# Another decoding of the float64 weights, and a new order of all steps, in a chunked-attention and gated-convolution kernel

## The chip, the cores and the metric

The kernel runs on one core of a Trainium2 chip. The core has five engines with a queue of instructions each: TensorE (PE, with its weight loads PEld), VectorE (DVE), ScalarE (ACT), GpSimd (POOL) and SyncE (SP, which only issues transfers). Each engine works through its queue in order and waits at an instruction until what it needs is there. Sixteen DMA engines move data between HBM and the core's memories. The metric is the device time of one execution in microseconds; lower is better.

## The reference

Two parts. The first is attention over q, k and v of shape (4 batches, 8 heads, 768 positions, 64). Each chunk of 32 queries sees 8 memory keys of its head, 16 keys to the left, its own 32 and 8 to the right, 64 in all. The second part takes the attention's output as x (4, 768, 512), makes a gate of a causal convolution with 5 taps and multiplies it with a matrix product:

```
scores = scale * q_c @ k_full.T;  a = exp(scores - max);  a = a / (sum(a) + 1e-9)
x[:, c] = a @ v_full                      # heads side by side: 512 columns
gate_pre = sum over k of conv_w[k] * x shifted by (4 - k) positions
out = (sigmoid(gate_pre) * (x @ w_val)) @ w_out
```

The inputs q, k, v, mem_k and mem_v are float32. The three weights w_val (512x512), conv_w (5x512) and w_out (512x512) are float64, so the kernel must make float32 values of them itself, from pairs of 32-bit words.

## The kernel before

**Units.** The attention is cut into 20 units: a unit is one pair of heads over one stretch of positions. Batch 0 has two stretches, of 256 and 512 positions (units 0 to 3 and 4 to 7); batches 1 to 3 have one of 768 each (units 8 to 11, 12 to 15, 16 to 19). For unit u the steps are: loads `lk`, `lq`, `lv`; transposes of k and q on PE (`tk`, `tq`) and their evictions (`ek`, `eq`); the scores (`sc`, PE, line 639); maximum, subtraction (`mx`, `ss`, DVE) and exponential (`ex`, ACT); transposes of the result (`tp`) and their evictions (`ep`); the product with v (`va`, PE, line 690); the division by the sum (`nd`, `ni`, `nx`, DVE, line 713 for `nx`); the transpose of the normalised x (`tx`); its split into a rounded part and the rest (`xh`, `xl`); five gate taps (`cv`, the first on ACT or DVE, lines 802 and 804, the others on DVE, line 798); and the tanh of the gate (`ga`, ACT). The tile of v is filled before its loads with the memory's rows (`mv`).

**Pieces.** The products with the weights go by 8 pieces of 256, 512 or 384 positions. `f1_n_co ci` is one block of x @ w_val of piece n, three matmuls (rounded x by rounded w, rounded x by the rest of w, the rest of x by rounded w; line 848). `h` (line 854) multiplies with the gate, `hh` and `hl` split the result, `f2_n_g ci` is one block of the product with w_out, again three matmuls (line 903), `oe` halves it and evicts it, and `st` stores it.

**Weights.** w_val and w_out come in four blocks of 128x512 float64 each, named wv0 to wv3 and wo0 to wo3, into two raw buffers (`lw`). Eight steps make a float32 block of a raw one: the exponent field (step 1, DVE, line 355), the mantissa field (2, DVE, 361), the low word added to it (3, DVE, 366), the exponent moved into place (4, ACT, 371), the mantissa as a number between 1 and 2 (5, ACT, 374), a clamp (6, DVE, 377), the sign (7, DVE, 382) and the product of both (8, POOL, 388). Then `h` makes the rounded part and the step without a suffix the rest. conv_w goes through the same eight steps once, as `cw1` to `cw8`.

**Order.** There is no scheduler at run time. A table, `ORDER`, lists every step with its engine (T is PE, V DVE, A ACT, G POOL, S SP), and the steps are emitted in this order; each engine's queue is what the table gives it. Buffers are counted, and a step that takes one waits for all users of the one that it replaces:

```
CAPS = dict(
    a=1, t=1, x=2, f=3, kn=2, qn=2, qT=2, ss=2, pT=2, xn=1, xh=4, xl=4, gate=5, h=2, hh=7, hl=7,
    o=3, ew=2, mw=2, wraw=2,
)
```

`wraw` is the raw weights, `ew` and `mw` the two work tiles of the decode, `kn` and `qn` the loaded k and q, `f` the PSUM banks of the products.

## Time and profile before

| | before |
|---|---|
| three timed runs, us | 267.76, 268.52 (median), 269.15 |
| span of the profiled execution, us | 269.1 |
| busy: PE, DVE, ACT, POOL, us | 238.3, 218.2, 127.9, 80.0 |
| instructions | 9694 |
| moved by DMA | 34.96 MB, mean 130 GB/s |

The span is the time from the first to the last instruction of one execution taken by the profiler; no other time of that execution is given, and the slowest of the timed runs is 0.05 us above it. The span is what a sum of durations is compared with, and it stands 0.6 us above the median of the timed runs.

Busy times are sums over the whole run, and this run has stages with different limits: DVE's share of the whole is 81%, and yet there are long stretches where it has no idle time, and others where it has much. So the windows are to be read, stage by stage. A group of instructions lists its count, its busy time and the mean of one. The chain follows the work that ended last back to what released it.

### The profile page before, as it was taken

Reading aid. Unit: us, or ns where it says so; the run is one execution under the profiler, and the core shown is the slowest. Engines: PE = TensorE matmul, PEld = TensorE weight load, DVE = VectorE, ACT = ScalarE, POOL = GpSimd, SP = SyncE. Lnnn points to the kernel's source line nnn. Section 1 sums busy time; section 2 is a strip of 40 time slices with the busy share of each in tenths; the row PEclk is TensorE's granted clock in tenths of the full one; section 3 lists DMA queues with packets and bytes.
Section 4 is the critical chain, followed back from the end, with each engine's and each line's share of the span. In section 5 each row is a group of like instructions: output and inputs, shape, how many; then the busy total and the mean of one; then the engine's idle time right before and its main releaser. Section 6 shows DMA issues by size and latency. Waiting matters only on the chain.

```text
span 269.1 us, 9694 instructions
## 1 busy us (share of the span) xinstructions
PE 238.3 (89%) x4158; PEld 200.2 (74%) x4158; DVE 218.2 (81%) x462; ACT 127.9 (48%) x259; POOL 80.0 (30%) x93
## 2 busy tenths in 40 slices
...
GB/s 151 177 198 207 211 178 183 117 210 180 177 137 147 144 186 178 44 132 137 165 164 132 160 149 55 106 163 187 101 143 2 4 168 44 80 0 39 78 48 111
DMA packets 99601, 34.96 MB, mean 130 GB/s; under 512 B 96082, under 2 KB 96358, under 8 KB 99558
## 3 DMA queue, kind: packets, MB, share of 16 engines
...
HBM read 28.03 MB, written 6.29 MB: 128 GB/s over the span
## 4 chain that ended last, share of the span: by engine, by line
PE 76%; DVE 12%; ACT 3%; issue 3%; DMA 3%; SPq 1%; POOL 1%; ACTq 0%; DVEq 0%
PE op L903 25%; PE vp L848 24%; PE sp L639 6%; PE xps L690 6%; PE tpx L750 4%; PE tq L569 4%; PE tk L569 4%; PE tp L569 4%; DVE gate L798 2%; DMA qn<-in_q_dram 2%; DVE e_wo L382 1%; DVE xn L713 1%; DVE e_wo L355 1%; SPq L493 1%; DMA craw<-in_moe_conv_w_dram 1%
## 5 line engine op out<-in xcount | busy, mean ns | idle before, releaser
L798 DVE SCALAR_TENSOR_TENSOR gate<-tpx,cw,gate 128x384 f32<-128x384 f32 (+9 forms) x144 | 79.3, 563 | 1.3 <-ACT gate L802 0.2
L264 POOL TENSOR_TENSOR hl<-h,hh 128x384 fp32r<-128x384 f32 (+2 forms) x25 | 26.0, 1044 | 107.6 <-DVE hh L249 55.2
L848 PE MATMUL vp<-xh,wv_hi 128*128 128x384 f32 (+2 forms) x128 | 49.1, 384 | 0.0
L848 PE MATMUL vp<-xl,wv_hi 128*128 128x384 f32 (+2 forms) x128 | 43.9, 343 | 0.0
L848 PE MATMUL vp<-xh,wv_lo 128*128 128x384 f32 (+2 forms) x128 | 43.9, 343 | 0.0
L903 PE MATMUL op<-wo_hi,hh 128*128 128x512 f32 (+1 forms) x100 | 41.9, 419 | 0.0
L903 PE MATMUL op<-wo_lo,hh 128*128 128x512 f32 (+1 forms) x100 | 38.6, 386 | 0.2 <-POOL wo_lo L264 0.2
L903 PE MATMUL op<-wo_hi,hl 128*128 128x512 f32 (+1 forms) x100 | 38.5, 385 | 0.0
L639 PE MATMUL sp<-kT,qT 64*32 64x64 f32 x1536 | 21.7, 239 | 8.7 <-DVE ss L664 3.9
L639 PEld LDWEIGHTS sp<-kT,qT 64*32 64x32 f32 x1536 | 17.6, 113 | 15.0 <-issue 8.4
L848 PEld LDWEIGHTS vp<-xh,wv_hi 128*128 128x128 f32 x128 | 25.0, 195 | 2.0
L854 DVE SCALAR_TENSOR_TENSOR h<-gate,vp 128x384 f32<-128x384 f32 (+2 forms) x32 | 17.2, 548 | 10.9 <-PE vp L848 9.4
L848 PEld LDWEIGHTS vp<-xh,wv_lo 128*128 128x128 f32 x128 | 25.1, 196 | 0.9
L848 PEld LDWEIGHTS vp<-xl,wv_hi 128*128 128x128 f32 x128 | 24.8, 194 | 0.9 <-DVE xl L264 0.2
L690 PE MATMUL xps<-v,pT 64*32 64x65 f32 x1536 | 21.1, 233 | 4.3 <-ACT pT L246 2.5
L690 PEld LDWEIGHTS xps<-v,pT 64*32 64x32 f32 x1536 | 17.3, 109 | 9.8 <-issue 6.1
L246 ACT COPY pT<-tp 128x384 f32<-128x384 f32 (+2 forms) x27 | 12.9, 479 | 23.5 <-PE tp L569 23.3
L569 PE MATMUL tk<-ident,kn 128*128 128x128 f32 x96 | 18.2, 304 | 6.2 <-ACT memT L246 2.6
L802 ACT ACTIVATE gate<-tpx,cw 128x384 f32<-128x384 f32 (+1 forms) x27 | 14.6, 549 | 15.1 <-PE tpx L750 10.0
L903 PEld LDWEIGHTS op<-wo_hi,hl 128*128 128x128 f32 x100 | 18.8, 188 | 4.0
L252 POOL COPY v<-mv 104x1536 f32<-104x1536 f32 (+2 forms) x12 | 17.4, 1458 | 11.5 <-issue 9.9
L569 PE MATMUL tq<-ident,qn 128*128 128x128 f32 x96 | 18.8, 311 | 2.1 <-DMA qn<-in_q_dram 0.9
...
## 6 DMA issues: line engine op xcount, KB each, us to landing
...
```

The lines of the kernel that those rows point to most:

```text
L246: return lambda: nc.scalar.copy(out(), in_())
L252: return lambda: nc.gpsimd.tensor_copy(out(), in_())
L264: return lambda: eng.tensor_tensor(out=out(), in0=a(), in1=b(), op=ALU.subtract)
L569: nc.tensor.transpose(U[name, i][:, (g - g0) * P : (g - g0 + 1) * P], src(g), ident)
L639: nc.tensor.matmul(U["sp"][CH * jc : CH * (jc + 1), j, g * WIN : (g + 1) * WIN], U["qT"][j * D : (j + 1) * D, g * P + CH * jc : g * P + CH ...
L690: nc.tensor.matmul(U["xps"][CH * jc : CH * (jc + 1), j, g * VW : (g + 1) * VW], U["pT"][j * D : (j + 1) * D, g * P + CH * jc : g * P + CH ...
L750: nc.tensor.transpose(U["x", i][:, o : o + P], U["xn"][:, g].rearrange("p j d -> p (j d)"), ident,)
L798: nc.vector.scalar_tensor_tensor(out=o, in0=i_, scalar=w, in1=o, op0=ALU.mult, op1=ALU.add)
L802: nc.scalar.activation(o, i_, AF.Copy, scale=w)
L848: nc.tensor.matmul(vp, w, x, start=ci == 0 and m == 0, stop=ci == NCT - 1 and m == 2)
L854: nc.vector.scalar_tensor_tensor(out=T["h", n, co][:, 0:nt], in0=bt[b, co]["gate"][:, t0 : t0 + nt], scalar=1.0, in1=T["vp", n, co][:, 0:n ...
L903: nc.tensor.matmul(op, x, w[:, ci, c0:c1], start=ci == 0 and m == 0, stop=ci == NCT - 1 and m == 2)
```

## The change

The decode has six steps in place of eight. The upper word of the float64, read as a float32, is scaled by a power of two and its absolute value is taken on ACT (`head`); two bounds are applied on DVE in one instruction; the bits are shifted left by 3 on DVE, which puts the exponent and the upper 20 bits of the mantissa in place; the sign is put in on DVE as before. The low word, scaled so that it fills the last three bits, is turned into an integer on ACT (`tail`) and added as an int32 on POOL. The two constant tiles and the steps `bias0` and `bias` are gone. What comes after the decode (`h`, the rest) is as it was.

```diff
+FLOOR = 2.0**-63
+CEIL = (1.875 - 2.0**-23) * 2.0**-32
...
-            nc.vector.tensor_scalar(
-                out=R["e"], in0=raw()[:, :, 1], scalar1=20, scalar2=0x7FF,
-                op0=ALU.logical_shift_right, op1=ALU.bitwise_and,
...
-                out=R["m"], in0=raw()[:, :, 1], scalar1=0xFFFFF, scalar2=None, op0=ALU.bitwise_and
...
-                out=R["mf"], in0=raw()[:, :, 0], scalar=2.0**-32, in1=R["m"], op0=ALU.mult, op1=ALU.add
...
-            nc.scalar.activation(R["ef"], R["e"], AF.Relu, bias=bias_e[0:np_], scale=E23)
-            nc.scalar.activation(R["mf"], R["mf"], AF.Identity, bias=one[0:np_], scale=2.0**-20)
-                out=R["e"], in0=R["ef"], scalar1=255 * E23, scalar2=None, op0=ALU.min
-            eng.tensor_tensor(out=R["mf"], in0=R["mf"], in1=R["ef"], op=ALU.mult)
+        def head():
+            nc.scalar.activation(
+                R["e"], raw()[:, :, 1].bitcast(F32), AF.Abs, scale=2.0**-48
+            )
+        def bounds():
+                out=R["e"], in0=R["e"], scalar1=FLOOR, scalar2=CEIL, op0=ALU.max, op1=ALU.min
+        def tail():
+            nc.scalar.activation(R["r"], raw()[:, :, 0], AF.Copy, scale=2.0**-29)
+        def shifted():
+                out=e, in0=e, scalar1=3, scalar2=None, op0=ALU.logical_shift_left
+        def signed():
+                out=e, in0=raw()[:, :, 1], scalar=0x80000000, in1=e,
+                op0=ALU.bitwise_and, op1=ALU.bitwise_or,
+        def rounded():
+                out=R["r"], in0=R["e"].bitcast(I32), in1=R["r"], op=ALU.add
...
-        step(name + "1", {"V": part1}, after=[load[0], "bias"], takes=bufs, uses=rawbuf)
+        step(name + "1", {"A": head}, after=[load[0]], takes=bufs, uses=rawbuf)
+        step(name + "2", {"A": tail}, after=[name + "1"], uses=rawbuf)
+        step(name + "3", {"V": bounds}, after=[name + "1"])
+        step(name + "4", {"V": shifted}, after=[name + "3"])
+        step(name + "5", {"V": signed}, after=[name + "4"], uses=rawbuf)
+        step(name + "8", {"G": rounded}, after=[name + "2", name + "5"], uses=bufs)
...
-G:ident V:bias0 S:mem A:bias S:lcw T:tmem A:lk0 V:cw1 A:cw4 A:emem01 S:lq1 A:emem00 V:emem11
+V:zv1 S:lw0 S:lcw S:mem A:cw1 V:zm V:cw3 V:cw4 V:cw5 A:wv01 V:wv03 G:ident T:tmem A:emem00 A:emem11
```

The whole table of the order is new, with the same steps otherwise: all movable steps may have another engine and another place. Two places are shown, as the engines' queues hold them.

PE in the opening, from the transposes of the probabilities of unit 0 on, before (`tp` and `xps` are a unit's transposes and value product, `tk` and `tq` transposes of k and q, `sp` scores, `tpx` the transpose of x, `vp` a product with w_val; the digit is the unit):

```order
L569 MATMUL tp0_0_245<-ident_67,ss0_194 128x128 x2
L690 MATMUL xps0_263<-v0_72,pT0_257 32x65 x16
L569 MATMUL tp1_0_285<-ident_67,ss1_248 128x128 x2
L569 MATMUL tk2_0_300<-ident_67,kn2_250 128x128 x3
L690 MATMUL xps1_308<-v1_73,pT1_293 32x65 x16
L750 MATMUL tpx0_0_325<-ident_67,xn0_295 128x128 x2
L569 MATMUL tq2_0_336<-ident_67,qn2_259 128x128 x2
L569 MATMUL tq3_0_359<-ident_67,qn3_288 128x128 x2
L639 MATMUL sp2_366<-kT2_70,qT2_339 32x64 x16
L750 MATMUL tpx1_0_388<-ident_67,xn1_349 128x128 x2
L569 MATMUL tk3_0_402<-ident_67,kn3_304 128x128 x3
L569 MATMUL tk4_0_409<-ident_67,kn4_342 128x128 x3
```

and further on in the same queue, at its first product with w_val:

```order
L690 MATMUL xps2_458<-v2_74,pT2_443 32x65 x16
L569 MATMUL tq5_0_481<-ident_67,qn5_351 128x128 x4
L569 MATMUL tp3_0_506<-ident_67,ss3_449 128x128 x2
L750 MATMUL tpx2_0_512<-ident_67,xn2_494 128x128 x2
L690 MATMUL xps3_522<-v0_72,pT3_509 32x65 x16
L569 MATMUL tq4_0_539<-ident_67,qn4_487 128x128 x4
L848 MATMUL vp0_1_546<-xh00_331,wv_hi_79 128x256
L848 MATMUL vp0_1_546<-xh00_331,wv_lo_80 128x256
```

The same place of the queue now:

```order
L550 MATMUL tp0_0_268<-ident_67,ss0_192 128x128 x2
L671 MATMUL xps0_273<-v0_72,pT0_271 32x65 x16
L550 MATMUL tp1_0_301<-ident_67,ss1_248 128x128 x2
L731 MATMUL tpx0_0_308<-ident_67,xn0_293 128x128 x2
L671 MATMUL xps1_312<-v1_73,pT1_306 32x65 x16
L550 MATMUL tk2_0_334<-ident_67,kn2_205 128x128 x3
L829 MATMUL vp0_0_342<-xh00_338,wv_hi_79 128x256
L829 MATMUL vp0_0_342<-xh00_338,wv_lo_80 128x256
L829 MATMUL vp0_0_342<-xl00_340,wv_hi_79 128x256
L731 MATMUL tpx1_0_360<-ident_67,xn1_356 128x128 x2
L550 MATMUL tq2_0_373<-ident_67,qn2_260 128x128 x2
L829 MATMUL vp0_1_380<-xh00_338,wv_hi_79 128x256
```

The first product with w_val stood behind the value product of unit 3 and stands now behind that of unit 1; the product of the next column block follows it before the scores of unit 2.

ACT in the opening before (`e_wv` and `m_wv` are the two work tiles of a decode, `raw_wv` the raw weights; L371 and L374 are steps 4 and 5, L672 the exponential of a unit, `kT`, `qT`, `pT` evictions of transposes):

```order
L371 ACTIVATE e_wv0_155<-e_wv0_155,bias_e_83 128x512
L246 COPY qT1_167<-tq1_0_159 128x256
L246 COPY cw_77<-tp_cw_197 128x20
L371 ACTIVATE e_wv1_170<-e_wv1_170,bias_e_83 128x512
L672 ACTIVATE ss0_194<-ss0_194 128x256
L246 COPY kT1_69<-tk1_0_213 128x12x2x16
L374 ACTIVATE m_wv0_156<-m_wv0_156,one_84 128x512
L246 COPY pT0_257<-tp0_0_245 128x256
L672 ACTIVATE ss1_248<-ss1_248 128x256
L246 COPY kT2_70<-memT_75 128x24x8
L246 COPY pT1_293<-tp1_0_285 128x256
```

and now (L347 is `head`, L357 is `tail`, L653 the exponential):

```order
L347 ACTIVATE e_wv1_140<-raw_wv1_132 128x512
L245 COPY qT0_155<-tq0_0_152 128x256
L357 ACTIVATE m_wv1_141<-raw_wv1_132 128x512
L245 CAST wv_hi_79<-m_wv0_104 128x512
L245 COPY cw_77<-tp_cw_208 128x20
L347 ACTIVATE e_wv3_211<-raw_wv3_199 128x512
L245 COPY kT1_69<-tk1_0_221 128x12x2x16
L653 ACTIVATE ss0_192<-ss0_192 128x256
L245 CAST wv_hi_79<-m_wv1_141 128x512
L357 ACTIVATE m_wv3_212<-raw_wv3_199 128x512
L245 COPY pT0_271<-tp0_0_268 128x256
L653 ACTIVATE ss1_248<-ss1_248 128x256
```

ACT's decode steps read work tiles that DVE wrote; now they read the raw weights, and the head of block 3 stands ahead of the eviction of k of unit 1 and of the exponential of unit 0, its tail ahead of the eviction of the probabilities of unit 0.

## Rows read from the trace of the kernel before

**Rows 1.** Windows: us, busy PE, PEld, DVE, ACT, POOL; clock; DMA share; GB/s

```profile
0.00:10.00 10.00, 2.73 (x8) 1.26 (x8) 4.29 (x11) 4.29 (x10) 6.91 (x22) 1.00 0.80 195
10.00:75.00 65.00, 48.23 (x946) 37.04 (x947) 62.10 (x143) 41.22 (x94) 29.78 (x26) 0.95 0.96 177
75.00:110.00 35.00, 32.89 (x814) 26.58 (x813) 30.94 (x67) 21.21 (x41) 9.34 (x9) 1.00 0.94 150
110.00:230.00 120.00, 119.09 (x2207) 103.32 (x2207) 104.29 (x213) 53.04 (x101) 27.84 (x30) 1.00 0.64 117
```

**Rows 2.** Timeline of DVE: start us, us, engine, line, operation, out<-in

```profile
118.33 0.96 DVE L713 TENSOR_TENSOR xn<-xps,den 128x768 f32<-128x768 f32 x1
```

**Rows 3.** Chain that ended last: start us, us, what

```profile
116.32 1.11 PE xps L690 x72
...
173.08 2.10 PE op L903 x9
...
233.47 11.51 PE vp L848 x66
```

**Rows 4.** Groups by line, DVE, decode: operation, count | busy us, mean ns | idle

```profile
L355 DVE TENSOR_SCALAR e_wv<-raw_wv 128x512 uint32<-128x512 uint32 x4 | 2.3, 574 | 0.0
...
L355 DVE TENSOR_SCALAR e_wo<-raw_wo 128x512 uint32<-128x512 uint32 x4 | 2.7, 687 | 0.0
...
L361 DVE TENSOR_SCALAR m_wv<-raw_wv 128x512 uint32<-128x512 uint32 x4 | 1.7, 415 | 0.0
...
L366 DVE SCALAR_TENSOR_TENSOR m_wv<-raw_wv,m_wv 128x512 f32<-128x512 uint32 x4 | 2.7, 679 | 0.0
...
L366 DVE SCALAR_TENSOR_TENSOR m_wo<-raw_wo,m_wo 128x512 f32<-128x512 uint32 x4 | 4.0, 1008 | 0.0
...
L382 DVE SCALAR_TENSOR_TENSOR e_wv<-raw_wv,e_wv 128x512 uint32<-128x512 uint32 x4 | 3.7, 916 | 0.0
...
L382 DVE SCALAR_TENSOR_TENSOR e_wo<-raw_wo,e_wo 128x512 uint32<-128x512 uint32 x4 | 5.4, 1356 | 0.0
...
L355 DVE TENSOR_SCALAR e_cw<-craw 20x128 uint32<-20x128 uint32 x1 | 1.3, 1333 | 2.3 <-DMA craw<-in_moe_conv_w_dram 2.3
```

**Rows 5.** Groups by line, steps that change engine or place

```profile
L804 DVE TENSOR_SCALAR gate<-tpx,cw 128x384 f32<-128x384 f32 (+1 forms) x9 | 5.1, 564 | 0.9 <-PE tpx L750 0.9
...
L249 DVE COPY kT<-tk 128x384 f32<-128x384 f32 x6 | 3.3, 557 | 2.0 <-PE tk L569 2.0
...
L249 DVE COPY v<-mv 104x1024 f32<-104x1024 f32 x1 | 3.0, 2966 | 0.0
...
L285 POOL MEMSET v<- 128x1560 f32 x3 | 4.2, 1395 | 0.0
...
L305 POOL MEMSET mv<- 128x1024 f32 x1 | 1.1, 1106 | 0.0
```

**Rows 6.** Timeline of DVE and POOL, 13 to 17 us

```profile
13.24 0.68 DVE L382 SCALAR_TENSOR_TENSOR e_wv<-raw_wv,e_wv 128x512 uint32<-128x512 uint32 x1
...
14.97 1.28 POOL L388 TENSOR_TENSOR m_wv<-m_wv,e_wv 128x512 f32<-128x512 f32 x1
...
15.18 1.62 DVE L382 SCALAR_TENSOR_TENSOR e_wv<-raw_wv,e_wv 128x512 uint32<-128x512 uint32 x1
```

**Rows 7.** Timeline, the last stores

```profile
265.77 0.81 SPq L944 DMA_DIRECT2D out_dram<-o  x2
```

**Rows 8.** DMA packets of the whole run, from the page

```profile
DMA packets 99601, 34.96 MB, mean 130 GB/s; under 512 B 96082, under 2 KB 96358, under 8 KB 99558
```

**Rows 9.** Groups by line, ACT and POOL, the decode

```profile
L388 POOL TENSOR_TENSOR m_wo<-m_wo,e_wo 128x512 f32<-128x512 f32 x4 | 5.2, 1296 | 3.6 <-ACT tpx L246 3.6
...
L371 ACT ACTIVATE e_wo<-e_wo,bias_e 128x512 f32<-128x512 uint32 x4 | 2.9, 732 | 0.0
...
L246 ACT CAST wo_hi<-m_wo 128x512 fp32r<-128x512 f32 x4 | 2.5, 626 | 0.0
```

**Rows 10.** Chain that ended last, the long transfer

```profile
16.09 4.77 DMA qn<-in_q_dram
```

More of the change, by code (lines that the diff above doesn't have):

```diff
@@ L12 @@
 U32 = mybir.dt.uint32
+I32 = mybir.dt.int32
 AF = mybir.ActivationFunctionType
@@ new lines @@
+S:lk1 V:ss0 A:wv0h G:wv0 S:lv0_1 S:lw3 S:lv0_0 S:lk2 T:tcw A:cw A:wv31 V:wv33 G:mk1 G:wv18 V:wv34
+V:wv35 S:lw2 T:tk1_0 A:ek1_0 A:ex0 A:wv1h T:sc1 V:mx1 V:ss1 A:wv32 S:lv1_1 S:lv1_0 V:mk2 S:lw5 S:lq2
+S:lk3 V:mk3 V:wv1 T:tp0_0 A:ep0_0 T:va0 V:nd0 V:ni0 V:nx0 G:wv38 A:ex1 A:wv21 V:wv23 T:tp1_0 V:wv24
+V:wv25 A:ep1_0 T:tx0_0 A:wv3h T:va1 V:nd1 S:lq3 T:tk2_0 A:xh0_0 V:xl0_0 T:f1_0_00 V:ni1 G:wv3
+V:cv0_0_4 A:wv22 A:ek2_0 G:wv28 A:wo11 V:nx1 V:cv0_0_0 V:cv0_0_1 T:tx1_0 V:hs1 A:xh1_0 A:cv1_0_4
+V:wo13 S:lmv S:lw4 T:tq2_0 A:eq2_0 A:wo12 V:wo14 T:f1_0_10 V:wv2h T:sc2 S:lk4 V:wo15 G:wv2 T:tq3_0
@@ new lines @@
+T:f2_1_11 V:ss11 A:oe1_2 S:lk12 T:tp10_1 A:ep10_1 A:ex11 T:f2_1_12 V:oe1_3 T:va10 T:tp11_0 T:f1_2_00
+V:xl9_1 A:ga8 V:cv9_1 A:ga9 A:mk15 V:nd10 V:ni10 T:f2_1_13 V:nx10 S:lv11_0 S:lv11_1 S:lk13 S:lq13
+S:lq14 A:ep11_0 T:tx10_0 V:cv10_0_4 A:xh10_0 T:tk12_0 A:ek12_0 V:cv10_0_0 T:f1_2_10 V:xl10_0 G:mv12
+V:cv10_0_1 A:oe1_1 T:tx10_1 T:tp11_1 A:ep11_1 T:f1_2_20 A:cv10_1_4 T:f1_2_11 T:va11 T:tk12_1
+V:cv10_0_2 A:xh10_1 V:cv10_1_0 V:cv10_0 T:f1_2_21 A:mk14 S:lk15 T:f1_2_01 V:nd11 A:mv13 A:ek12_1
+V:xl10_1 T:f1_2_22 V:ni11 V:cv10_1_1 V:nx11 T:f1_2_02 T:tx11_0 A:cv11_0_4 S:lv12_1 S:lv12_0 T:tk13_1
@@ L232, in tile_chunked_attention_gated_conv @@
     wo_lo = const.tile([P, NCT, DM], F32R, name="wo_lo")
-    bias_e = const.tile([P, 1], F32, name="bias_e")
-    one = const.tile([P, 1], F32, name="one")
-    ones = const.tile([P, 1], F32, name="ones")
     plan = Plan(dict(CAPS))
@@ L264, in minus @@
         return lambda: eng.tensor_tensor(out=out(), in0=a(), in1=b(), op=ALU.subtract)
-    def biases():
-        nc.vector.memset(bias_e, -896 * E23)
-        nc.vector.memset(ones, 1.0)
-    E23 = 2.0**23
     step("ident", {"G": lambda: make_identity(nc, ident)})
-    step("bias0", {"V": biases})
-    step("bias", {"A": lambda: nc.scalar.copy(one, ones)}, after=["bias0"])
     def zero_k(eng):
@@ L385, in part7 @@
             )
-        def part8(eng):
-            eng.tensor_tensor(out=R["mf"], in0=R["mf"], in1=R["ef"], op=ALU.mult)
+        def rounded():
+            nc.gpsimd.tensor_tensor(
+                out=R["r"], in0=R["e"].bitcast(I32), in1=R["r"], op=ALU.add
+            )
         rawbuf = load[1]
-        step(name + "1", {"V": part1}, after=[load[0], "bias"], takes=bufs, uses=rawbuf)
-        step(name + "2", {"V": part2}, after=[name + "1"], uses=rawbuf)
-        step(name + "3", {"V": part3}, after=[name + "2"], uses=rawbuf)
@@ L394, in float64_steps @@
-        step(name + "4", {"A": part4}, after=[name + "1"])
-        step(name + "5", {"A": part5}, after=[name + "3"])
-        step(name + "6", {"V": part6}, after=[name + "4"])
-        step(name + "7", {"V": part7}, after=[name + "6"], uses=rawbuf)
-        step(
-            name + "8",
-            {"G": lambda: part8(nc.gpsimd), "V": lambda: part8(nc.vector)},
-            after=[name + "5", name + "7"], uses=bufs,
-        )
+        step(name + "1", {"A": head}, after=[load[0]], takes=bufs, uses=rawbuf)
```

226 lines of the change are left out of this document (102 added, 124 removed).

## The prediction

> **What bounds the kernel now.** I read the stage windows first [rows 1]. Three stages show. From 10 to 75 us VectorE (DVE) is busy 62.1 of 65 us, while TensorE (PE) has 48.2 and the DMA engines have a share of 0.96 at 177 GB/s. From 75 to 110 us DVE has 30.9 of 35 us, PE 32.9 and DMA 0.94. From 110 to 230 us PE has 119.1 of 120 us, DVE 104.3, and DMA drops to 0.64. So the first 110 us belong to DVE, with the DMA engines close behind it, and the rest belongs to PE. ScalarE (ACT, 41.2 of 65 us) and GpSimd (POOL, 29.8) have room in every stage, but they run their queues in order and can still hold somebody up.
>
> A second reading fixes where the first stage ends for the sum. I take as its mark the last DVE step of unit 11, the normalisation nx11, which starts at 118.33 us [rows 2]; by then both batches 0 and 1 have been through attention. On PE the mark is the value product of unit 11, va11, at 116.3 us [rows 3]. A DVE that is hardly ever idle up to there makes the time of nx11 the sum of the DVE instructions queued ahead of it. After it PE runs with no hole: 66 products of 384 columns take 11.51 us and 9 products of 512 columns take 2.10 us [rows 3], which is 0.52 us for an f1 step (three products) and 0.70 us for an f2 step.
>
> **The change on DVE.** For each of eight 128x512 weight pieces three DVE instructions go: the exponent field (L355), the mantissa field (L361) and the low word's product (L366). From [rows 4] they are 2.3 + 2.7 us, 8 x 0.415 = 3.3 us, and 2.7 + 4.0 us, together 15.0 us. The bounds take the place of the old clamp (L377), an instruction of one source and two constants like it, and the sign (L382) stays as it is: nothing for both. The left shift is new: one source and one constant, as L361 is, so 8 x 0.415 = 3.3 us more. The convolution weights lose the odd first instruction, 1.3 us [rows 4].
>
> The new order moves other things between engines. I counted the steps that stand ahead of nx11 on DVE in both orders. The fill of v by DVE goes, 3.0 us; eight more gate taps come (five first ones that ACT did, three later ones moved forward), 8 x 0.56 = 4.5 us; the zero fills of one v tile and of mv come from POOL, where they took 1.4 and 1.1 us, 2.5 us; of the smaller steps (casts, evictions, oe) one more comes than goes, 0.5 us at the kT eviction's price [rows 5]. How DVE fills zeros in such tiles no row shows: between 0 and those 2.5 us, since they stand at the start, where DVE waits anyway; I keep 2.5.
>
> Sum on DVE up to nx11: -15.0 + 3.3 - 1.3 - 3.0 + 4.5 + 2.5 + 0.5 = -8.5 us.
>
> **The change on PE.** By va11 the new order has done four f1 steps and five f2 steps more than the old one: 4 x 0.52 + 5 x 0.70 = 5.6 us of PE work that no longer stands behind nx11, because the first weights are decoded early and the products of piece 0 start in the middle of the attention of units 0 to 3, where PE has holes. In the old queue the first product stands behind four value products, in the new one behind two. As PE is full after the mark, this comes off the end.
>
> **What takes some back.** (a) Part of the 15.0 us is stretch: L355 took 0.574 and 0.687 us against 0.415 for L361, L366 1.008 against 0.679 [rows 4], and that is 4 x 0.16 + 4 x 0.27 + 4 x 0.33 = 3.0 us. The L382 at 13.24 took 0.68 us and the one at 15.18, with a POOL L388 running from 14.97, took 1.62 [rows 6]: DVE stands while POOL works on its own operands. POOL has the same work, so the stretch may fall on other DVE instructions. Between 0 and 3.0; I charge 1.5. (b) DMA: the loads issued through the v tile of unit 11 are 17.3 MB in the old order and 17.8 MB in the new (counted from the steps). At the pace of [rows 1] the queues deliver 1.95 MB in the first 10 us, 11.5 to 75 us and 0.15 MB a us after, which makes 17.8 MB at about 104 us, and va11 now wants it at 116.3 - 8.5 = 107.8. The margin is 4 us for all waits for free buffers together; I charge 2, with 0 and 6 as its ends. (c) The tail: the last output is now a full 512-column half-scale and a 256 KB store where it was a 256-column one. The last store's issue is at 265.77 [rows 7]; I charge 0.4.
>
> The Trainium skill, "DMA: Bandwidth & Descriptors", Specifications, gives about 358 GB/s of HBM for a core; by it 17.8 MB would take an estimated 50 us and (b) would be nothing, 2 us less in the sum. The trace does not agree: 150 to 177 GB/s at a share of 0.94 to 0.96, and it counts 96082 of 99601 packets under 512 B [rows 1, 8]. The same section asks for 512 B and more for line rate, and by that the trace agrees. I go by the rows.
>
> **Costs without a row.** The int32 addition on POOL: nearest is the float product that it replaces, 1.296 us [rows 9]; it could be from about half of it to the 2.97 us of the slowest elementwise row [rows 5]. POOL is idle more than half of the first 75 us, so the eight cost nothing there but delay; on the path stand one or two, 0 to 3 us. I take 1.3 us each and no charge. ACT reads every second word of raw and takes an absolute value, or writes int32: nearest are 0.732 us for L371 and 0.626 us for a plain cast [rows 9]; DVE shows no price for the same stride (0.415 on raw). Sixteen before, sixteen after: 0 to -1.7 us on an engine with room, no charge.
>
> Total: 269.1 - 8.5 - 5.6 + 1.5 + 2.0 + 0.4 = 258.9 us of span. The page's span is 269.1 us and the median of the three runs is 268.52, 0.6 less, so the forecast is 258.3 us.
>
> **The rivals.**
> 1. The pulled products are no gain: they only trade places with waits, since PE is not quite free of them (DVE 104.3 of 120 us beside it). Then only the DVE term counts: 258.3 + 5.6 = 264 us. For it: PE's order is new everywhere, so other holes may open. Against: 119.1 of 120 us busy after the mark. Chance 0.18.
> 2. DMA is the bound of the first stage already (share 0.96 and 0.94). One late transfer held the chain for 4.77 us [rows 10]. Then va11 stays where DMA lets it, near 114, and the front gives 2 instead of 8.5 - 1.5 - 2.0 = 5 us: 261 to 262 us. Chance 0.10.
> 3. Slower: ACT heads wait for weights. In the new order the first step of each decode is on ACT and reads the DMA's buffer, and copies that PE waits for stand right behind it: the head of wv3 is ahead of the kT eviction and the exponential of unit 0. Before, ACT's decode waited only for DVE. Only two weight buffers exist, and SP's queue holds the later k, q and v loads behind each weight load that waits for a buffer. Eight heads; if each holds ACT for more than 10.2 / 8 = 1.3 us of chain, the gain is gone; at the 4.77 us of [rows 10] for half of them it is 19 us and the time 277. Against: the loads of wv0 and wv1 are issued first of all. Chance 0.07.
> 4. Slower: DVE's stretch. If all 24 DVE instructions of the new decode took the 1.62 us of [rows 6], they would need 39 us where I count 3.3 + 3.3 + 9.1 = 15.7 [rows 4], and the time would be 281; from 10.2 / 24 = 0.43 us of extra stretch each the change is a loss. Against: POOL's busy time is no greater than before, and in the old kernel 16 of the same kind ran at 0.415. Chance 0.05. "GPSIMD Engine Reference", Key points, of the Trainium skill says that GpSimd shares its SBUF interfaces with VectorE and contends with instructions that use both ports or have two SBUF inputs, which all three new ones may be; the two L382 of [rows 6] agree.
> 5. The change does nothing that can be measured, because a wait in the opening (rival 3 in small) eats the front. 268 us. Chance 0.05.
>
> **How the numbers follow.** The forecast has 0.55; its own range is 252 to 264 (the ends: all stretch back +1.5, DMA 6 instead of 2 for +4; below, no charge for (a) and (b), and the zero fills free, -6). A measurement of this kernel can tell about 0.5%, 1.3 us, from no change. Faster by more than that are the forecast, rivals 1 and 2: 0.83. Rival 5 with what lies between: 0.07. Slower are most of rivals 3 and 4: 0.10. The range for 8 in 10 runs from 250.5 us to 266.5: it leaves out rivals 3 to 5 and a little at the low end.
>
> **What would show it.** Right: DVE's start of nx11 some 8 us earlier (near 110 us) and va11 on PE with it, L366's group gone, the sign's mean still 0.9 to 1.4 us, PE full after about 105 us. Wrong: idle time of ACT before the head, released by a DMA, with PE waiting for kT or pT behind it (rival 3); bounds and shift above 0.8 us (rival 4); POOL additions above 2 us; waits of PE for DMA between 60 and 110 us (rival 2); or PE holes after 110 us of more than 5 us (rival 1).

## The result and the profile after

| | before | after |
|---|---|---|
| timed runs, us | 267.76 to 269.15, median 268.14 of 4 | 270.65, 270.80, 270.80, 271.55, median 270.80 |
| ratio to before | | 1.0106, interval 1.0075 to 1.0138 |
| span of the profiled execution, us | 269.1 | 268.9 |
| busy: PE, DVE, ACT, POOL, us | 238.3, 218.2, 127.9, 80.0 | 237.5, 209.8, 130.9, 74.6 |

The changed kernel is slower by 1.1%, where 258.3 us, 3.8% faster, was forecast. The spans are nearly the same, which needs a word: in all runs that give both figures, the time stands 1.7 to 2.1 us above the span. The profiled execution of before (269.1) therefore lasted about 270.9 us, above every timed run in the table; the one of after (268.9) belongs to the run of 270.65. So the 0.6 us that the forecast set between span and timed median is no fixed distance. It loses nothing by that, since 10.2 us taken from the span or from the median of 268.5 give the same 258.3. But the two profiles compare a run of before that was some 2.4 us slower than its median with an ordinary run of after. In the experiments below a time is the median of all runs of a kernel, and a ratio compares those runs of each that lie within 1.5% of its fastest.

The windows of after, in the four stretches of [rows 1], with the same columns:

```profile
0.00:10.00 10.00, 1.32 (x4) 0.68 (x4) 5.23 (x12) 4.23 (x9) 3.74 (x18) 1.00 0.72 192
10.00:75.00 65.00, 50.79 (x966) 37.74 (x967) 55.51 (x130) 37.36 (x85) 33.04 (x32) 0.97 0.83 173
75.00:110.00 35.00, 33.81 (x723) 25.76 (x722) 32.71 (x70) 19.15 (x41) 9.33 (x9) 1.00 0.87 152
110.00:230.00 120.00, 116.87 (x2283) 99.76 (x2281) 101.37 (x196) 59.59 (x115) 21.33 (x21) 1.00 0.66 117
```

DVE fell from 62.1 to 55.5 us between 10 and 75, as it should, but nothing came forward for it: DVE now stands idle for 9.5 of these 65 us, where it did for 2.9. DMA's share fell too. Behind 110 us PE has 3.1 us of holes where it had 0.9, and in the first 10 us PE does 1.3 us of work instead of 2.7. The mark of the forecast, nx11 on DVE and va11 on PE, answers to [rows 2, 3]:

```profile
117.79 1.18 PE L671 MATMUL xps<-v,pT 64*32 64x65 f32 x96
...
120.19 0.94 DVE L694 TENSOR_TENSOR xn<-xps,den 128x768 f32<-128x768 f32 x1
```

nx11 starts 1.9 us later (118.33 before), not 8.5 earlier. The decode's groups, which answer to [rows 4, 9], with L352 the bounds, L361 the shift, L367 the sign, L373 the addition and L347 the head:

```profile
L373 POOL TENSOR_TENSOR m_wo<-e_wo,m_wo 128x512 int32<-128x512 int32 x4 | 5.1, 1279 | 4.1 <-ACT wo_hi L245 2.5 <-DVE e_wo L367 1.6
...
L352 DVE TENSOR_SCALAR e_wv<-e_wv 128x512 f32<-128x512 f32 x4 | 3.9, 974 | 1.0 <-ACT e_wv L347 1.0
...
L361 DVE TENSOR_SCALAR e_wv<-e_wv 128x512 uint32<-128x512 uint32 x4 | 3.8, 951 | 0.1
...
L361 DVE TENSOR_SCALAR e_wo<-e_wo 128x512 uint32<-128x512 uint32 x4 | 3.1, 782 | 0.0
...
L367 DVE SCALAR_TENSOR_TENSOR e_wv<-raw_wv,e_wv 128x512 uint32<-128x512 uint32 x4 | 2.8, 698 | 0.1
...
L367 DVE SCALAR_TENSOR_TENSOR e_wo<-raw_wo,e_wo 128x512 uint32<-128x512 uint32 x4 | 2.7, 682 | 0.0
...
L347 ACT ACTIVATE e_wo<-raw_wo 128x512 f32<-128x512 f32 x4 | 2.7, 672 | 0.0
...
L352 DVE TENSOR_SCALAR e_wo<-e_wo 128x512 f32<-128x512 f32 x4 | 2.1, 526 | 0.6 <-ACT e_wo L347 0.6
```

Bounds, shift and sign take 6.0 + 6.9 + 5.5 = 18.4 us where the forecast had 15.7; the five DVE steps of the old decoding (L355, L361, L366, L377, L382) took 27.7. The **stretch**, the time by which a DVE instruction is longer beside a POOL instruction than alone, has moved: the sign, 1.36 and 0.92 us before, is at 0.69, and the shift, forecast at 0.415, is at 0.95 and 0.78.

The opening shows both a late start and a stretched decode ahead of the softmax. The timeline from 7 to 16 us (start, length, engine, line, operation, in brackets the idle time ahead and what ended it):

```profile
7.14 0.45 PE L316 MATMUL tp_mem<-ident,mk_nat 128*128 128x128 f32 x1 [7.14 <-DMA mk_nat<-in_mem_k_dram]
...
10.08 1.27 POOL L373 TENSOR_TENSOR m_wv<-e_wv,m_wv 128x512 int32<-128x512 int32 x1 [1.16 <-DVE e_wv L367]
10.32 2.64 DVE L352 TENSOR_SCALAR e_wv<-e_wv 128x512 f32<-128x512 f32 x1
...
11.29 1.40 POOL L277 MEMSET v<- 128x1560 f32 x1
...
11.70 0.68 PE L620 MATMUL sp<-kT,qT 64*32 64x64 f32 x32 [0.55 <-ACT qT L245]
...
12.82 1.26 POOL L263 TENSOR_TENSOR wv_lo<-m_wv,wv_hi 128x512 fp32r<-128x512 f32 x1
13.00 1.36 DVE L361 TENSOR_SCALAR e_wv<-e_wv 128x512 uint32<-128x512 uint32 x1
...
14.40 0.71 DVE L367 SCALAR_TENSOR_TENSOR e_wv<-raw_wv,e_wv 128x512 uint32<-128x512 uint32 x1
...
15.30 0.42 DVE L641 TENSOR_REDUCE mx<-sp 128x4 f32<-128x256 f32 x1
```

The first transpose waits until 7.14 us for mk_nat, which is issued behind a 512 KB weight. The scores of unit 0 are done at 12.4 us, but their maximum (L641) starts at 15.30, because bounds, shift and sign of the second weight stand ahead of it, and the bounds last until 12.96, through a POOL addition and a memset that ends at 12.69.

To compare orders in which different PE work stands ahead of a step, I use PE's **slack**: the start of a step less the PE work queued ahead of it, at the prices of stretches in which PE has no hole (0.52 us for an f1 step of 384 columns, 0.70 for f2, 1.10 for scores or value product of 768 rows as in [rows 3], 0.78 of 512, 0.50 of 256, a transpose step 0.19 to 0.36). Slack grows by what PE waits or loses; the difference of two kernels' slack at the end is the difference of their ends. The profiled runs differ somewhat in the granted clock (0.95 from 10 to 75 us in before and e1, 0.97 in after, 1.00 in e14 and e16, 0.83 from 30 to 50 us in e15), so a difference of a microsecond up to va9 says little.

| slack, us, at | va1 | va9 | va11 | va14 | va16 | end |
|---|---|---|---|---|---|---|
| before | 15.0 | 46.1 | 50.4 | 55.4 | 57.5 | 60.5 |
| new decoding, old order (e1) | 14.4 | 44.6 | 46.5 | 51.4 | 53.4 | 56.7 |
| after | 19.9 | 42.3 | 46.6 | 51.7 | 56.5 | 60.1 |
| after, old order from va13 (e7) | 19.1 | 41.5 | 45.8 | 52.5 | 54.6 | 57.9 |
| weights nearly free, old order (e14) | 14.3 | 38.4 | 40.5 | 45.8 | 47.9 | 51.2 |
| weights nearly free, new order (e15) | 16.5 | 36.0 | 40.3 | 45.4 | 50.3 | 53.9 |
| e1 with three moves (e16) | 15.4 | 41.8 | 43.6 | 48.5 | 50.6 | 53.8 |

### The profile page after: what moved, and what is told of

It is laid out like the page before. It is cut to its first block, busy times and chain, and to the rows that moved or that the text cites. A ratio compares the mean times of both kernels' runs of the same rounds, so it can differ in the third digit from the quotient of the medians.

```text
span 268.9 us, 9674 instructions
## 1 busy us (share of the span) xinstructions
PE 237.5 (88%) x4158; PEld 195.3 (73%) x4158; DVE 209.8 (78%) x433; ACT 130.9 (49%) x267; POOL 74.6 (28%) x88
## 4 chain that ended last, share of the span: by engine, by line
PE 57%; DVE 28%; ACT 6%; issue 5%; DMA 2%; SPq 0%; ACTq 0%; DVEq 0%
PE vp L829 19%; PE op L884 17%; DVE gate L779 10%; PE xps L671 5%; PE sp L620 4%; PE tk L550 3%; PE tp L550 3%; PE tpx L731 3%; PE tq L550 3%; DVE mx L641 2%; DMA mk_nat<-in_mem_k_dram 2%; DVE xl L263 2%; DVE xn L694 2%; DVE h L835 2%; DVE gate L785 2%
## 5 line engine op out<-in xcount | busy, mean ns | idle before, releaser
L779 DVE SCALAR_TENSOR_TENSOR gate<-tpx,cw,gate 128x384 f32<-128x384 f32 (+8 forms) x144 | 79.5, 565 | 5.4 <-ACT gate L783 2.2
L263 POOL TENSOR_TENSOR hl<-h,hh 128x384 fp32r<-128x384 f32 (+2 forms) x25 | 25.4, 1019 | 107.0 <-ACT hh L245 69.7
L829 PE MATMUL vp<-xl,wv_hi 128*128 128x384 f32 (+2 forms) x128 | 44.6, 348 | 0.3 <-DVE xl L263 0.3
L251 POOL COPY v<-mv 104x1536 f32<-104x1536 f32 (+2 forms) x14 | 18.5, 1319 | 37.4 <-PE xps L671 25.4
L245 ACT COPY pT<-tp 128x384 f32<-128x384 f32 (+2 forms) x31 | 14.8, 478 | 21.8 <-PE tp L550 21.3
L245 ACT COPY qT<-tq 128x384 f32<-128x384 f32 (+2 forms) x31 | 15.0, 484 | 17.9 <-PE tq L550 17.8
L245 ACT CAST xh<-tpx 128x384 fp32r<-128x384 f32 (+1 forms) x31 | 13.6, 443 | 18.8 <-PE tpx L731 8.2
L620 PEld LDWEIGHTS sp<-kT,qT 64*32 64x32 f32 x1536 | 16.6, 108 | 7.4 <-issue 2.2
L620 PE MATMUL sp<-kT,qT 64*32 64x64 f32 x1536 | 20.0, 230 | 2.1 <-ACT qT L245 0.8
L550 PE MATMUL tq<-ident,qn 128*128 128x128 f32 x96 | 17.8, 296 | 3.6 <-ACT qT L245 2.6
```

The costliest lines, as they stand in the source:

```text
L245: return lambda: nc.scalar.copy(out(), in_())
L251: return lambda: nc.gpsimd.tensor_copy(out(), in_())
L263: return lambda: eng.tensor_tensor(out=out(), in0=a(), in1=b(), op=ALU.subtract)
L550: nc.tensor.transpose(U[name, i][:, (g - g0) * P : (g - g0 + 1) * P], src(g), ident)
L620: nc.tensor.matmul(U["sp"][CH * jc : CH * (jc + 1), j, g * WIN : (g + 1) * WIN], U["qT"][j * D : (j + 1) * D, g * P + CH * jc : g * P + CH ...
L779: nc.vector.scalar_tensor_tensor(out=o, in0=i_, scalar=w, in1=o, op0=ALU.mult, op1=ALU.add)
```

## The experiments

Ratios are to the kernel before, timed beside each run on the same chip, with 95% intervals in brackets; a ratio of two experiments is worked out from these, its interval with the two taken as independent. 1% is 2.7 us. The order table wraps differently in them, so line numbers stand some lines lower (bounds L348, shift L357, sign L363).

**Decoding and order apart (e1, e2).** Each new decoding step at the place of the old one in the old order, and the reverse:

```diff
 in the order of before, for each weight x (e1)
-V:x1 V:x2 V:x3 A:x4 A:x5 V:x6 V:x7
+A:x1 A:x2 V:x3 V:x4 V:x5
 in the order of after (e2)
-A:x1 A:x2 V:x3 V:x4 V:x5
+V:x1 V:x2 V:x3 A:x4 A:x5 V:x6 V:x7
```

> The new decoding (head and tail on ACT, bounds, shift and sign on DVE, integer addition on POOL) put into the order of the kernel before, each new step at the place of the old one that it answers to; nothing else differs from before. Theory O (the decoding is worth what the forecast said, and the new order loses it again by its late opening and by waits of its own): DVE loses about 10 us of work in a front in which it was never idle, so nx11, at 118.33 us before, starts 5 to 10 us earlier and the time is 260 to 265 us, faster than both kernels. Rival D (the decoding itself buys nothing here, because PE, DMA or ACT is next in line at once): nx11 moves by less than 2 us and the time is 267 to 270 us. Rival S (the decoding is a loss: heads on ACT and DVE's stretch beside POOL): over 271 us.

> The old decoding put into the order of the changed kernel: exponent, mantissa and low product on DVE where the head stood on ACT, with ACT's exponent scaling in the head's place; the rest of the order is that of the changed kernel. Theory O: this carries the late opening and the order's own waits and has no gain on DVE, so it is the slowest of the four: 274 to 282 us. Rival D: the decoding matters in neither order, so the time is that of the changed kernel, 269 to 272 us. Rival S: without the new decoding the new order shows its gain, 262 to 267 us.

e1: 266.98 us, ratio 0.9969 (0.9931 to 1.0007). e2: 276.65 us, ratio 1.0352 (1.0296 to 1.0407). So the decoding is worth 0.3% in the old order (-0.1 to 0.7, not clear of nothing) and 1.0352 to 1.0106, 2.4% (1.8 to 3.0), in the new one; the new order costs 3.5% with the old decoding and 1.0106 / 0.9969, 1.4% (0.9 to 1.9; 3.7 us), with the new one. Theory O has the signs right in both, and the size wrong in e1: it expected 260 to 265, and the time is nearer to rival D's 267 to 270. The durations of all DVE instructions ahead of nx11 sum to 117.7 us before and 104.9 in e1, 12.8 less. These durations overlap, since the next instruction's record often begins before the last one's ends; the windows up to nx11, before and in e1, tell how long DVE was busy at all:

```profile
0.00:118.33 118.33, 92.17 (x1900) 71.86 (x1901) 105.05 (x236) 70.71 (x152) 51.06 (x62) 0.97 0.89 162
```

```profile
0.00:114.41 114.41, 90.83 (x1900) 71.11 (x1901) 95.23 (x215) 69.03 (x151) 49.80 (x62) 0.97 0.81 168
```

Busy time fell by 9.8 us, from 105.05 to 95.23, and idle time rose from 13.3 to 19.2, so nx11 starts only 3.9 us earlier, and by as much do the two profiled spans differ (269.1 and 265.2); the waits are new:

```profile
114.41 0.96 DVE L690 TENSOR_TENSOR xn<-xps,den 128x768 f32<-128x768 f32 x1
```

```profile
DVE sp L633 <- PE sp L616: 2.7, 2, 1.6
DVE den L683 <- PE xps L667: 1.7, 3, 1.2
DVE gate L775 <- ACT xh L241: 1.1, 1, 1.1
DVE xl L259 <- ACT xh L241: 1.0, 2, 0.6
DVE gate L781 <- ACT xh L241: 0.9, 1, 0.9
```

These are DVE's waits in e1 from 10 to 75 us (total, times, longest): for scores, for value products, for ACT's copies. Before, the same list has 0.8, 0.6, 0.2 and 0.2 us. Once DVE had room, it waited for steps of PE and ACT, which in their turn follow earlier steps of DVE.

**The opening (e3 to e6, e8).** Four edits try to take back the late start: the small loads first (e3), the second weight's DVE steps behind the softmax besides (e4), the heads of both weights behind the copies too (e5), and the whole opening of the old order (e6).

```diff
-S:lw0 S:lcw S:mem A:cw1
+S:mem S:lcw S:lq0 S:lk0 S:lw0 A:cw1
 e4: besides
-V:ek0_0 V:wv13 V:wv14 V:wv15
+V:ss0 V:wv13 V:wv14 V:wv15
 e5: the heads too
+A:eq0_0 A:wv01 A:wv02
+V:ss0 A:ex0 V:wv03 V:wv04 V:wv05 G:wv08 A:wv11 A:wv12 V:wv13 V:wv14 V:wv15
 e6: order of e1 up to T:va1, then what is left in the order of after
```

> The changed kernel with four loads of SP's queue (mem, lcw, lq0, lk0) issued ahead of the first weight (lw0); nothing else differs. In the changed kernel PE's first transpose waits until 7.14 us for mk_nat. Theory O, part opening: the transpose starts near 3 us, scores of unit 0 near 9 us instead of 11.70, va0 2 to 3 us earlier than 20.15, and if nothing later absorbs it the time falls by 2 to 3 us, to about 268. Rival A (absorbed: DVE, which has the weights' steps ahead of the softmax, or the waits near 62 and 170 us set the end): va0 earlier, but the time stays within 1 us of 270.8.

> As the run before (four small loads first), and DVE's bounds, shift and sign of the second weight (wv13, wv14, wv15) stand behind the first softmax step (ss0) instead of ahead of it. In the changed kernel they took 2.64, 1.36 and 0.71 us there and held mx0 until 15.30 us, with the scores done at 12.4. Theory O, part opening: mx0 starts right behind the scores, near 10 us, va0 near 15.5 to 16.5 us as before the change (15.5), and 4 to 5 us come off the end: 266 to 267 us. Rival A: va0 is 4 us earlier, va6 and va11 are not, and the time is 269 to 271.

> The changed kernel with a repaired opening: the four small loads ahead of the first weight, and besides the first two weights' heads and tails on ACT behind the copies that PE waits for (after eq0_0, and after ex0), their DVE steps behind the first softmax step; all the rest as changed. Theory H (the opening loses its time because the head of the first weight stands on ACT ahead of memT's copy, so that with small loads first the head waited for raw_wv until 9.91 us and with the weight first mk_nat came at 7.14): tk0 starts near 5 us, va0 near 15 instead of 20.2 us, and PE's slack (start of a product less the PE work ahead of it) at va11 is some 4 us below the changed kernel's 46.6. If that reaches the end the time is 266 to 268 us. Rival A (the opening is absorbed, since later weights are late by as much): va0 near 15 us, but slack at va7 and va11 within 1.5 us of the changed kernel's, time 269.5 to 272.

> New decoding; the order of the kernel before up to va1 (as in the run of the new decoding in the old order), and then whatever is left in the order of the changed kernel. Theory H: as the run before, with va1 near 17.8 us and a time of 265 to 268 us. Rival A: 269 us or more, since the weights that the changed order wants by then have not been decoded and the first products wait.

None was faster than the changed kernel: 272.37 us, 1.0176 (1.0115 to 1.0237); 271.66 us, 1.0154 (1.0095 to 1.0214); 272.43 us, 1.0155 (1.0112 to 1.0197); and 275.14 us, 1.0249 (1.0212 to 1.0286). Theories O and H on the opening fall by their times. But the first three did not even bring va0 forward: it starts at 22.99, 21.61 and 21.39 us against 20.15 in the changed kernel, where 15 to 18 had been expected, so they do not tell what an early opening would be worth. In e3 the wait only changed places. ACT's timeline there:

```profile
3.00 0.32 ACT L343 ACTIVATE e_cw<-craw 20x128 f32<-20x128 f32 x1 [0.98 <-DMA craw<-in_moe_conv_w_dram]
9.91 0.66 ACT L343 ACTIVATE e_wv<-raw_wv 128x512 f32<-128x512 f32 x1 [6.58 <-DMA raw_wv<-in_moe_w_val_dram]
10.47 0.42 ACT L241 COPY memT<-tp_mem 64x64 f32<-64x64 f32 x2
```

The transpose was done at 3.3 us, but its copy (memT) stands behind the head of the first weight, which waits 6.58 us for that weight. This is rival 3, as it was described, in one place: tk0 came at 11.7 us instead of 8.8. In e5 the head was out of the way, and the cw copy then stood behind a cast that waited for POOL:

```profile
15.20 0.62 ACT L241 CAST wv_hi<-m_wv 128x512 fp32r<-128x512 f32 x1 [1.38 <-POOL m_wv L369]
...
15.72 0.17 ACT L241 COPY cw<-tp_cw 128x20 f32<-128x20 f32 x1
...
15.95 0.90 PE L546 MATMUL tk<-ident,kn 128*128 128x128 f32 x3 [3.68 <-ACT cw L241]
```

In e6, where a few steps behind va1 also had to stand some places off, va1 was early (17.6 us), and slack is 31.6 us at va2, against 25.8 in the changed kernel: PE waited 9.17 us for the cast of unit 0's x on ACT, which stood behind a head that waited 5.99 us for its weight. In the new order an early opening was paid for by later weights in the one splice that had it; that no other opening could be early and have its weights ready is not shown.

**The back (e7, e8, e12).** The new order up to a step, and from there what is left in the old order:

```diff
 e7:  order of after up to T:va13, then what is left in the order of e1
 e12: order of after up to T:va11, then what is left in the order of e1
 e8:  as e7, with the opening of e5
```

> The changed kernel's order up to va13, and then whatever is left in the order of the kernel before. PE's slack grows between va13 and the end by 9.9 us in the changed kernel and by 7.4 and 7.6 us in the old order with old and new decoding. Theory B (the new order of the last 120 us makes 2 to 3 us of waits of its own): the growth falls to 7 to 8 us and the time to 268 to 269. Rival W (the waits come because the products that could fill them were done earlier: work pulled forward is missing later, in whatever order): the growth stays at 9.5 us or more, the time at 270.5 to 271.5.

> The changed kernel's order up to va11 instead of va13, then what is left in the order of the kernel before. From va11 to the end PE's slack grew by 13.5 us in the changed kernel, by 10.1 and 10.2 us in the old order, and by 12.1 us with the old order from va13 on. Theory B: the rest of the loss lies between va11 and va13, the growth is 10 to 11 us and the time 267 to 268 us. Rival W (the waits of this stretch come from work that was pulled ahead): growth 12 us or more, time 268.5 to 270 us.

> Both edits: the repaired opening and, from va13 on, what is left in the order of the kernel before. Theories H and B together: 4 us and 2 to 3 us come off, 263 to 266 us, faster than both kernels. If only H holds, 266 to 268; if only B, 268 to 269; if neither, 270 to 272.

e7: 268.94 us, ratio 0.9998 (0.9962 to 1.0034), 1.1% (0.6 to 1.5) below the changed kernel. Theory B holds by the time, and nearly by slack, which grows by 8.4 us behind va13 instead of 9.9 (7 to 8 expected). Where, the windows show; 30 us from va14 on in the changed kernel, and the same part in e7:

```profile
165.00:195.00 30.00, 28.01 (x533) 24.61 (x521) 24.39 (x48) 14.63 (x29) 5.48 (x5) 1.00 0.75 136
```

```profile
162.00:192.00 30.00, 30.00 (x626) 26.39 (x625) 28.03 (x58) 15.34 (x27) 6.30 (x7) 1.00 0.70 134
```

PE is full in e7 and has 2 us of holes in the changed kernel, whose chain there, from 175.6 to 188.4 us, holds no PE at all but turns between ACT and DVE (start, length, what):

```profile
179.14 0.62 DVE gate L779
...
180.91 0.59 ACT gate L783
...
181.52 0.63 DVE gate L779
...
183.48 0.46 DVE h L835
...
186.45 0.97 DVE mx L641
...
187.44 0.97 DVE ss L645
```

The table shows it as slack from va14 to va16: 4.8 us in after and 4.9 in e15, 2.0 to 2.1 in every kernel with the old order there. e12: 269.99 us, 1.0057 (1.0014 to 1.0101); the old order from va11 on gets back less. Slack grows by 12.9 us, as rival W had it; 5.4 of it lie between va11 and va12, where after has 2.8, so PE loses at the seam itself. e8: 270.60 us, 1.0089 (1.0058 to 1.0120), the time expected if neither theory held: behind the opening of e5 the old back gets back 0.7% (0.1 to 1.2), no more than in e7.

**What the decoding still costs (e9, e10).** In e9 DVE's three steps of e1, in e10 POOL's addition of the changed kernel work on one column:

```diff
 e9, the same for all three
-out=R["e"], in0=R["e"], scalar1=FLOOR, scalar2=CEIL
+out=R["e"][:, 0:1], in0=R["e"][:, 0:1], scalar1=FLOOR, scalar2=CEIL
 e10
-out=R["r"], in0=R["e"].bitcast(I32), in1=R["r"]
+out=R["r"][:, 0:1], in0=R["e"][:, 0:1].bitcast(I32), in1=R["r"][:, 0:1]
```

> New decoding in the old order (as the first run), but bounds, shift and sign work on one column of 512 instead of on all: DVE's decoding of the eight weights is left out but for one column, so the weights are not the reference's. It takes 12 us (eight times 0.42, 0.42 and 0.69) and the stretch beside POOL, some 18 us in all, from DVE before nx11. Theory L (since the first removal of 12.8 us brought nx11 forward by 4 us only and DVE waited for the rest, the front is now a chain of handovers between engines and not DVE's sum): nx11 starts at 108 to 112 us instead of 114.4, DVE's idle time ahead of it grows from 9.5 to more than 20 us, time 261 to 265 us. Rival V (DVE's sum still decides): nx11 near 100 us, time 250 to 256 us. Rival N (nothing left in it): time 266 to 268 us.

> The changed kernel, but POOL's integer addition of each weight works on one column of 512: the last bits are left out but for one column, so the weights are not the reference's. The order and every other instruction are as changed. If POOL at work is what stretches DVE (in the changed kernel the shift took 0.42 to 0.43 us where no POOL instruction ran beside it and 1.05 to 1.38 us beside one), bounds and shift fall from means of 0.75 and 0.87 us towards 0.42 to 0.5 (the residues wv_lo and wo_lo still run on POOL). Theory L: the time falls by no more than 2 us, to 268.5 to 270.5, since the steps are not where PE waits. Rival 4 of the forecast (the stretch decides): 4 us or more, 266 or less.

e9: 263.76 us, 0.9814 (0.9755 to 0.9872), 1.6% (0.9 to 2.2) below e1: another 12.9 us of DVE work ahead of nx11 (104.9 to 92.0) give some 4 us (2 to 6). Theory L holds by the time but not by its mark: it expected nx11 at 108 to 112 us, and in the profile, of a run 2.7 us above the median, nx11 stands at 114.73, no earlier than in e1, with DVE busy for 82.4 us up to there. e10: 267.53 us, 0.9943 (0.9899 to 0.9987), 1.6% (1.1 to 2.1) below the changed kernel, about 4.3 us: my theory L (no more than 2) fails by the ratio, and rival 4 of the forecast (4 or more) is near it. The granted clock is not the same in the two, though. Half of e10's runs had 0.999 to 1.00 (264.25 to 266.68 us) and half 0.980 to 0.994 (268.38 to 269.61); no run of the changed kernel was above 0.994 (270.65 to 271.55). So part of the 4.3 us may be the clock. The groups of e10:

```profile
L348 DVE TENSOR_SCALAR e_wv<-e_wv 128x512 f32<-128x512 f32 x4 | 2.8, 696 | 1.0 <-ACT e_wv L343 1.0
...
L357 DVE TENSOR_SCALAR e_wo<-e_wo 128x512 uint32<-128x512 uint32 x4 | 2.5, 622 | 0.0
...
L357 DVE TENSOR_SCALAR e_wv<-e_wv 128x512 uint32<-128x512 uint32 x4 | 1.7, 427 | 0.1
...
L369 POOL TENSOR_TENSOR m_wv<-e_wv,m_wv 128x1 int32<-128x1 int32 x4 | 0.7, 187 | 4.9 <-DVE mx L637 3.0 <-ACT e_wv L343 1.2 <-DVE den L683 0.7
```

The shift of w_val is back from 0.951 to 0.427 us, and each block is ready 1.1 us sooner. Which of the two brings the gain stays open: the addition was not moved, only shrunk. The old decoding had a POOL product of the same length [rows 9], so this is no cost of the new decoding alone.

**Is it the transfers, and is the order a gain when weights are cheap? (e13 to e15).** e13 is e1 with six of eight weight loads cut to 64 columns. e14 and e15 are the old and the new order with that cut, and those of e9 and e10.

```diff
-T["raw", c] = buf([P, DM, 2], "wraw", f"raw_{name}", U32)
-eng.dma_start(T["raw", c], w[ci * P : (ci + 1) * P, :]...)
+T["raw", c] = raws[len(loaded) % 2]
+n = DM if len(loaded) < 2 else DM // 8
+eng.dma_start(T["raw", c][:, 0:n], w[ci * P : (ci + 1) * P, 0 : 2 * n]...)
```

> New decoding in the old order, but six of the eight weight loads (all but the first two) bring 64 of 512 columns: 2.7 of 17.3 MB are left out, the decoding works on whatever the buffer held before, and the weights are not the reference's. All instructions of the engines are as in the first run. Theory Q (with DVE relieved the front waits for transfers next: in the run with DVE's decoding cut the chain of the first 72 us held 13.0% of kn loads and 10.1% of v loads): fewer bytes in the queues bring va7 1.5 to 3 us forward, time 263.5 to 265.5. Rival N (transfers wait for buffers and issues, not for bandwidth): 266 to 268 us, as with the full loads.

> Old order, new decoding with nearly all its cost left out: bounds, shift, sign and POOL's addition on one column of 512, and six of the weight loads cut to 64 columns. ACT's heads and tails, the casts and the residues stay. Cutting DVE's share alone brought 3.2 us (267.0 to 263.8). Theory L: a little more, 260 to 263 us, since about 25 us of DVE work gone (against the kernel before) return some 6 to 8 us. Rival V: 254 us or less.

> The same cuts in the order of the changed kernel. This tells what the new order is worth when the weights cost next to nothing. Theory P (the products pulled forward are a gain as forecast, but the changed kernel pays for it by decoding four weights ahead of the first softmax): the new order now beats the old one of the run beside it by 2 to 5 us, 256 to 260 us. Rival T (they only trade places with waits, and the new order loses 2 to 4 us in the last 150 us whatever the weights cost): 2 to 4 us above the old order, 263 to 267 us.

e13: 266.46 us, 0.9949 (0.9904 to 0.9994), against 0.9969 for e1: 2.7 MB less change nothing that can be measured. Rival N holds; in the old order bandwidth is not the next limit. e14: 260.00 us (258.52 to 264.13), 0.9713 (0.9639 to 0.9786), as its theory L had it. e15 beside it on the same chip: 263.76 us (262.18 to 264.90), 0.9853 (0.9786 to 0.9921). Rival T holds: with the decoding nearly gone the new order still costs 1.4% (0.4 to 2.5), 3.8 us, as much as with the whole of it.

**A better version (e11, e16).** PE's longest wait in e1 is 4.02 us for ss4, behind a triple of DVE's decoding that POOL stretches. DVE and POOL there:

```profile
35.48 1.27 POOL L259 TENSOR_TENSOR wv_lo<-m_wv,wv_hi 128x512 fp32r<-128x512 f32 x1
...
35.76 1.26 DVE L357 TENSOR_SCALAR e_wo<-e_wo 128x512 uint32<-128x512 uint32 x1
36.69 1.23 POOL L247 COPY v<-mv 104x1024 f32<-104x1024 f32 x1
37.06 1.41 DVE L363 SCALAR_TENSOR_TENSOR e_wo<-raw_wo,e_wo 128x512 uint32<-128x512 uint32 x1
...
40.21 1.05 PE L616 MATMUL sp<-kT,qT 64*32 64x64 f32 x64 [4.02 <-DVE ss L641]
```

```diff
 e16: e1 with
-V:wo03 ... V:wo04 V:wo05 V:mx4
+V:ss5 V:wo03 V:wo04 V:wo05
+V:nx5 V:wo13 V:wo14 V:wo15
+V:ss7 V:wo23 V:wo24 V:wo25
 e11: besides
-A:lk1
+S:lk1 S:lw0
```

> New decoding in the old order with four moves: bounds, shift and sign of the first w_out piece behind ss5 instead of ahead of mx4 (there they took 1.33, 1.28 and 1.41 us and PE waited 4.02 us for ss4), those of the second behind nx5, those of the third behind ss7, and unit 1's key load on SP's queue ahead of the first weight instead of late on ACT's (PE waited 2.07 us for it). Theory L: PE's waits at 11.4 (2.07 us), 40.2 (4.02), 52.3 (2.18) and 63.3 us (1.39) shrink and half of that reaches the end: 262 to 264.5 us, faster than both kernels. Rival A (the waits only move to the next handover): 265.5 to 267.5 us.

> The full new decoding in the old order with the three moves of DVE's steps behind ss5, nx5 and ss7, and without the move of unit 1's key load (which had put the first weight's load behind it: its head waited until 12.30 us and held the cw copy, and va0 came at 16.6 instead of 14.9 us). Theory L: the early 1.7 us are back, a part reaches the end: 263.5 to 265.5 us. Rival A (absorbed by the next wait): 265.5 to 267 us.

e11: 265.91 us, 0.9904 (0.9863 to 0.9945), in the range of its rival A; its first heads waited 4.46 and 0.90 us for weights that now come later. e16, without that move: 264.20 us, 0.9879 (0.9833 to 0.9925): faster than before by 1.2%, than the changed kernel by 2.2% (1.7 to 2.8) and than e1 by 0.9% (0.3 to 1.5), with the same instructions as e1. Not all of this is shown to be the moved steps as such. PE's clock from 40 to 44 us, first in e1, behind the wait of 4.02 us, then in e16, where that wait is 0.70 us:

```profile
40.00:44.00 4.00, 3.79 (x79) 3.65 (x79) 3.45 (x9) 2.44 (x5) 0.00 (x0) 0.57 1.19 160
```

```profile
40.00:44.00 4.00, 2.13 (x75) 1.76 (x74) 3.04 (x9) 1.97 (x5) 1.26 (x1) 1.00 1.19 154
```

In e1 PE ran for most of these 4 us at the lower of its two levels (1.2 GHz), in e16 throughout at the upper one (2.4 GHz). Ten of the twelve runs of e16 had a mean clock of 0.997 or more, two of those of e1. At 0.986 to 0.987 two runs of e16 took 266.54 and 268.07 us and seven of e1 266.31 to 268.41; at 0.997 or more the ten of e16 took 262.65 to 266.46 and the two of e1 265.29 and 265.93. The shorter wait and the clock that stays up came together, and no run tells them apart.

## Why the prediction was wrong, point by point

**The step that failed** is in its second paragraph: "A DVE that is hardly ever idle up to there makes the time of nx11 the sum of the DVE instructions queued ahead of it." DVE was idle for 13.3 of the 118.33 us; [rows 1] alone show 5.7, 2.9 and 4.1 us of it. That its durations, 117.7 us in sum, nearly equal the start of nx11 is luck: their overlap, 12.7 us, happens to match the idle time. And the front is a ring of handovers through queues that run in order, scores to maximum to exponential to transposition to value product: what DVE gained it waited for the others. Taking 12.8 us off DVE's durations gave 0.8 us of time (e1, with an interval of -0.2 to 1.9), the next 12.9 gave some 4 (e9); 8.5 had been booked in full.

**The change on DVE.** The 12.8 us of e1 lie near the forecast for the decode, 15.0 - 3.3 + 1.3 = 13.0, by luck too. The decode's own steps lost 10.3, because bounds and shift took 11.5 us, where the old clamp's 3.5 and 3.3 for the shift had been reckoned, and the sign 1.7 less than before; 2.3 came from the fill of v, at 0.69 instead of 2.97 us. In the changed kernel DVE's sum ahead of nx11 fell by only 5.4 us, to 112.3: the decode's steps lost 10.8 instead of 13.0, and the other moves brought 5.4 instead of 4.5. Busy time fell by 2.8 us, idle time rose from 13.3 to 17.9, and nx11 moved by +1.9:

```profile
0.00:120.19 120.19, 95.79 (x1929) 72.39 (x1930) 102.24 (x228) 69.18 (x149) 47.20 (x60) 0.99 0.79 160
```

**The change on PE.** "As PE is full after the mark, this comes off the end": this failed too, and e14 and e15 show it with the weights out of the way. The table tells how, from e1 to after. The late opening costs 5.5 us of slack by va1. From va1 to va9 PE waits less, as the pulled products were meant to bring about, and 7.8 us come back. From va9 to va11 the new order loses 2.4 (slack grows by 4.3, as before the change, against 1.9 in e1; no run shows why), and from va14 to va16 2.8 more, behind the chain of ACT and DVE shown with e7. Rival 1 had the mechanism ("they only trade places with waits") and put it at no gain; with its opening and its back the order is a loss of 3.7 us.

**What takes some back.** (a) Stretch was undersized. The 1.5 us charged are 2.7 by the groups, and POOL's addition as a whole is worth up to some 4 us of the changed kernel's time (e10). (b) The 2.0 us for DMA were not needed: its share fell to 0.83 and 0.87, PE waited for no transfer between 60 and 110 us, and e13 shows no effect in the old order. (c) The tail: the last product ends 3.9 us ahead of the span's end, and 3.7 before, 0.2 where 0.4 was charged.

**The rivals.** 2 (DMA) falls. 3 is shown as a mechanism in e3 (6.58 us in one head), but in the changed kernel the heads waited for no weight. 5 (the opening eats the front) was right for the opening, and had the smallest chance beside 4. None of them put the late opening and the lost back together, and so the time lies between rival 5's 268 us and the 277 and 281 of rivals 3 and 4.

**What would show it.** nx11 near 110 us: no, 120.19. The sign at 0.9 to 1.4 us: no, 0.69, with the shift at 0.8 to 0.95, which the text gave as the sign of rival 4. PE holes of more than 5 us behind 110: no, 3.1 up to 230. L366's group gone: yes.
